# The first batch's front regrouped by heads and half tiles in an eight-batch linear-attention and mixer kernel

## The chip, the cores and the metric

The kernel runs on one core of a Trainium2 chip. The metric is the device time of one execution in microseconds; runs of one kernel agree within about 0.1%. In a profile PE is the matrix engine, PEld its weight loads, DVE, ACT and POOL are the vector, scalar and general-purpose engines, SP only issues DMAs. Engines run their own instruction lists in order and meet through semaphores.

## What is computed

Eight batches, eight heads, 576 rows, head dimension 64: linear attention with a cosine/sine weight, then a token mixer and a channel mixer. All inputs and the output are float32; the kernel multiplies in bf16.

```python
r = relu(q); q_p = concat([r*cos_w, r*sin_w], -1)   # the same for k: k_p
kv  = einsum('bhsf,bhsd->bhfd', k_p, v)
z   = sum(k_p, axis=2)
x   = einsum('bhsf,bhfd->bhsd', q_p, kv) / (einsum('bhsf,bhf->bhs', q_p, z) + 1e-6)
x   -> (B, 576, 512)                                  # heads side by side
u   = x + (relu(x^T @ w_tok1) @ w_tok2)^T             # 576 -> 256 -> 576
out = u + relu(u @ w_ch1) @ w_ch2                     # 512 -> 1536 -> 512
```

## The kernel before

The 576 rows of a batch are four chunks of 128 (`ci` 0 to 3, R = 4) and a tail of 64 rows; the tails of two batches share one tile of 128. For each batch there is a *front* (attention and token mixer) and a *channel* stage (`c_main` L540, matmuls with w_ch1, L546; `o_step` L572, matmuls with w_ch2, L579). The order of every engine is written out by hand. From batch 1 on, the pieces of a front are set between the steps of the channel stage of the batch before, by a list of (step, piece) that `pieces` (L461) makes: KS and QS make the features of k and q (L261 on ACT, L263 on DVE), V casts values to bf16 (L274 to L276), KV the product k_p^T v (L320), N the numerator (L359) and its division (L367 to L369), `u` the second token matmul (L406). In batch 2 and later the transposes of q run as DMA transposes on SP's queue (`q_trans_dma` L348, issue L350).

The front of batch 0 (`first_front`, L636) has nothing to hide behind. It goes, in PE's order:

- 12 filler matmuls (`busy`, L204: zeros times the identity into a tile nobody reads), then the transposes of q (L340) for heads 0 to 3 and then 4 to 7, each copied to SBUF by ACT (L344), then the tail of q;
- for k: features, two fillers, `ksum` (L285: eight one-column matmuls a chunk), chunk by chunk; ACT makes half of the features of chunks 2 and 3; then `ksum_out` (L293, ACT);
- `dens` (L302), the denominators of three chunks; `kv` for heads 0 to 3; `dens` of the other two; `kv` for heads 4 to 7. `kv_out` (L331) copies the low half on ACT and the high half on DVE;
- `num` (L359) with the division on DVE (L369, one instruction a chunk) two chunks ahead of `tok1` (L382, two matmuls a chunk); ACT casts w_tok1 (L207) and reorders w_tok2 (L210, L212) meanwhile;
- relu into B (L387, L389), the transposed u (L425, L433), its copies (L707), and the first channel matmuls (L556).

PSUM pools: `ps_mm` with four tiles of one bank, `ps_at` with two tiles of two banks. `kv` of each half takes a `ps_at` tile.

Loads. SP issues q heads 0-3 (L105), then the tail of q, k in two halves, the tail of k, v heads 0-3, the tail of v, v heads 4-7, w_tok1, w_tok2; ACT issues q heads 4-7 at the same time as SP's first. SP's and ACT's loads share eight semaphores in turn, so each load from the ninth on also waits until the load eight before it has landed. POOL issues the casting loads: the tail rows of w_tok1, then w_ch1 in four pieces (L188), the first of which waits for k's second half (L192). Batch 1's k, v and q (L736) wait for the second piece of w_ch1. w_ch2 comes in three pieces of four chunks (L196), which stand in POOL's list behind and between two casts of batch 1's values. Batch 2's loads of v and of all tails (L762, L763) are issued late in batch 0's channel stage and stand on SP ahead of two output stores and of batch 2's DMA transposes.

Of the kernel before, what the change touches and what calls it, by code (L numbers as in the profile page):

```python
# [16 lines left out]
def kernel(  # L17
# [87 lines left out]
    load_main(qt0, q, 0, HH, H, nc.scalar)  # L105
    load_tail(qtt0, q, 0)
    load_main(kt0, k, 0, 0, HH)
    k_done = load_main(kt0, k, 0, HH, H)
# [3 lines left out]
    load_main(vt0, v, 0, HH, H)  # L112
# [3 lines left out]
    w_tok1n = stage1[:, 0:R * D_tok].rearrange("p (r t) -> p r t", r=R)  # L116
    w_tok2n = stage2[:, 0:NT * S].rearrange("p (n s) -> p n s", n=NT)
    nc.sync.dma_start(out=w_tok1n, in_=moe_w_tok1[0:SM, :].rearrange("(p r) t -> p r t", r=R))
    nc.sync.dma_start(out=w_tok2n, in_=moe_w_tok2.rearrange("(n t) s -> t n s", t=P))
# [35 lines left out]
    v_augs, x_tails = [], []  # L155
    for i in range(2):
        va = const.tile([P, NSC, H, DP], BF16, name=f"v_aug{i}")
        nc.vector.memset(va[:, 0:R, :, D:D1], 1.0)
        nc.vector.memset(va[half(1 - i), R, :, :], 0.0)
        nc.vector.memset(va[half(i), R, :, D:D1], 1.0)  # L160
        v_augs.append(va)
        xt = const.tile([P, Dm], BF16, name=f"x_tail{i}")
        nc.vector.memset(xt[half(1 - i), :], 0.0)
        x_tails.append(xt)
# [15 lines left out]
    for t in (tail0.kp, tail0.qp):  # L180
        nc.gpsimd.memset(t[half(1)], 0.0)
    for g in range(2):
        nc.gpsimd.dma_start(out=w_tail1[half(g), :], in_=moe_w_tok1[SM:S, :])
# [8 lines left out]
    after(w_ch1_done[0], k_done)  # L192
    w_ch2_done = []
    def load_w_ch2(third):
        ki = third * NCH // 3
        w_ch2_done.append(nc.gpsimd.dma_start(  # L196
            out=w_ch2[:, ki:ki + 4, :],
            in_=moe_w_ch2[ki * P:(ki + 4) * P, :].rearrange("(n t) d -> t n d", t=P)))
# [10 lines left out]
    def permute_tok2(ki):  # L209
        nc.scalar.copy(w_tok2[:, ki, 0:SM].rearrange("t (r p) -> t r p", r=R),  # L210
                       w_tok2n[:, ki, 0:SM].rearrange("t (p r) -> t r p", r=R))
        nc.scalar.copy(w_tok2[:, ki, SM:].rearrange("t (g s) -> t g s", g=2),  # L212
                       w_tok2n[:, ki, None, SM:S].to_broadcast([P, 2, ST]))


    class Front:
        def __init__(self, b, res, tail):
            self.qt, self.vt, self.kt = io_tiles[b]
            self.va, self.xt = v_augs[b % 2], x_tails[b % 2]
            self.res, self.tail = res, tail  # L220
            self.rows = half(b % 2)


            self.alone = b < 2
            self.kp, self.qp = {}, {}

            self.qpT = once.tile([P, R * H, P], BF16, name="qpT")
            self.kv_sb = [twos.tile([P, HH, DP], BF16, name=f"kv_sb{g}") for g in range(2)]
            self.x = once.tile([P, R, Dm], BF16, name="x_sb")
# [65 lines left out]
        def dens(self, ci):  # L295

            if ci == 0:
                self.d_ps = ps_mm.tile([P, NSC * H], F32, name="d_ps", tag="mm")
                self.d_sb = small.tile([P, NSC * H, 1], F32, name="d_sb")
            for h in range(H):  # L300
                i = ci * H + h
                nc.tensor.matmul(self.d_ps[:, i:i + 1], self.qT_of(ci, h),  # L302
                                 self.ks_sb[:, h:h + 1], start=True, stop=True)

        def dens_out(self, lo, hi):
            nc.vector.tensor_scalar_add(self.d_sb[:, lo:hi, 0], self.d_ps[:, lo:hi], 1e-6)
            nc.vector.reciprocal(self.d_sb[:, lo:hi, 0], self.d_sb[:, lo:hi, 0])

        def kv(self, ci, halves=(0, 1)):
            if ci == 0 and not hasattr(self, "kv_ps"):  # L310
                self.kv_ps = {}
                if halves == (0, 1):
                    both = ps_at.tile([P, 2, 512], F32, name="kv_ps", tag="at")
                    self.kv_ps = {g: both[:, g, :] for g in range(2)}
            if ci == 0 and halves != (0, 1):
                for g in halves:
                    self.kv_ps[g] = ps_at.tile([P, 2, 512], F32, name="kv_ps", tag="at")[:, 0, :]
            for g in halves:
                for j in range(HH):
                    nc.tensor.matmul(self.kv_ps[g][:, j * DP:j * DP + D1],  # L320
                                     self.k_of(ci)[:, g * HH + j, :, :]
                                     .rearrange("p a b -> p (a b)"),
                                     self.va[:, ci, g * HH + j, 0:D1],
                                     start=(ci == 0 and j == 0),
                                     stop=(ci == NSC - 1 and j == HH - 1),
                                     skip_group_check=True)

        def kv_out(self, halves=(0, 1)):
            for g in halves:
                copy = nc.vector.tensor_copy if g else nc.scalar.copy  # L330
                copy(self.kv_sb[g][:, :, 0:D1],  # L331
                     self.kv_ps[g][:, 0:HH * DP]
                     .rearrange("p (j d) -> p j d", d=DP)[:, :, 0:D1])
# [13 lines left out]

        def q_trans_dma(self, ci):  # L348
            dst = self.qpT[:, ci * H:(ci + 1) * H, :] if ci < R else self.tail.qpT
            nc.sync.dma_start_transpose(out=dst,  # L350
                                        in_=self.q_of(ci).rearrange("p h a b -> p (h a b)"))

        def num(self, ci, fill=0, dens=False):
            num_ps = ps_at.tile([P, 2, 512], F32, name="num_ps", tag="at")
            if fill:
                busy(num_ps[:, 0, HH * DP:512], 1)
            for h in range(H):
                g, j = divmod(h, HH)
                nc.tensor.matmul(num_ps[:, g, j * DP:j * DP + D1], self.qT_of(ci, h),  # L359
                                 self.kv_sb[g][:, j, 0:D1], start=True, stop=True)  # L360
            rows = self.rows_of(ci)
            nv = num_ps[rows, :, 0:HH * DP].rearrange("p g (j d) -> p g j d", d=DP)
            if dens:
                den = self.d_sb[rows, ci * H:(ci + 1) * H, :].rearrange("p (g j) o -> p g j o", g=2)
            else:
# [3 lines left out]
            nc.vector.tensor_mul(  # L369
                self.x_of(ci)[rows].rearrange("p (g j d) -> p g j d", g=2, j=HH),  # L370
                nv[:, :, :, 0:D], den.to_broadcast([rows.stop - rows.start, 2, HH, D]))
# [89 lines left out]
        def pieces(self, b, before):  # L461
# [7 lines left out]
            if first:  # L469

                u, act, pool = before.tok2, nc.scalar, nc.gpsimd
                plan = [(4, KS, 0), (4, KS, 1), (5, u, 0, ps_at, False), (5, KS, 2, True),
                        (6, KS, 3, True), (6, u, 1, ps_at, False), (7, KS, R), (7, V, R, nc.vector), (8, V, 0, act),
                        (8, V, 2, pool), (8, load_w_ch2, 0), (8, V, 3, pool),
                        (8, load_w_ch2, 1), (8, load_w_ch2, 2),
                        (8, u, 2, None, False), (9, V, 1, act), (9, u, 3, None, False),
                        (9, QS, 0), (10, u, R, None, False)]
# [6 lines left out]
            else:  # L484
                plan = [(C + at, V, ci, nc.scalar)
                        for ci, at in enumerate((6, 6, 7, 7, 7) if late else (-1, -1, 0, 1, 2))]
# [10 lines left out]
                for at, side, ci in sides:  # L497
                    plan.append((C + at, side, ci))
                    if side == QS:
# [3 lines left out]
                         enumerate((7, 7, 8, 8, 8) if late else  # L503
# [28 lines left out]
    class Channel:  # L532
# [59 lines left out]
        def steps(self, done):  # L592
# [24 lines left out]
            if self.b == 0:  # L617

                for lo in range(0, NCH, 4):
                    for ci in (0, 1):  # L620
                        o_range(ci, lo, lo + 4)
# [14 lines left out]
    def first_front(f):  # L636
# [4 lines left out]
        busy(idle_ps, 12)  # L641
# [10 lines left out]
        f.q_side(R)  # L652
        f.q_trans(R, pool=ps_at)
        busy(idle_ps, 2)
        for ci in range(R):
            f.feature("k", ci, 0)
            f.feature("k", ci, 1, on_act=(ci > 1))
            busy(idle_ps, 2)
# [4 lines left out]
        busy(idle_ps, 1)  # L663
        for ci in range(R):
            if ci == 2:
                f.ksum_out()
            f.values(ci, nc.scalar, lo_heads)
        cast_tok1(0)
        f.values(R, nc.vector)
        for ci in range(R):  # L670
            f.values(ci, nc.vector, hi_heads)
        for ci in (0, 1, 2):
            f.dens(ci)
# [3 lines left out]
        for ci in (R, 3):  # L677
            f.dens(ci)
        f.dens_out(0, NSC * H)
        for ci in range(NSC):  # L680
            f.kv(ci, (1,))
        f.kv_out((1,))
        cast_tok1(1)
        for ki in range(NT):
            permute_tok2(ki)
# [3 lines left out]
        f.num(ORDER[0], fill=1, dens=True)  # L689
        f.num(ORDER[1], dens=True)  # L690
        for i, ci in enumerate(ORDER):
            if i + 2 < NSC:
# [55 lines left out]
    for b in range(B):  # L748
# [4 lines left out]
        for i, step in enumerate(steps):  # L753
# [5 lines left out]
            if b == 0 and i == NCH:  # L759
                load_batch(2, "kq", behind=w_ch2_done[1], tails=False)  # L760
            if b == 0 and i == NCH + 13:
                load_batch(2, "v", tails=False)  # L762
                load_batch(2, "kqv", main=False)  # L763
# [44 lines left out]
```

## Time and profile before

| what | us |
|---|---|
| median of 3 runs (range) | 269.88 (269.80 to 269.96) |
| the profiled execution, its time | 270.61 |
| its span, first to last instruction | 268.8 |
| PE busy in the span | 260.0 (97%), 2029 matmuls |
| DVE, ACT, POOL busy | 164.9, 129.9, 10.9 |
| first channel matmul (L556) starts | 24.45 |
| DMA: moved, mean rate | 53.68 MB, 200 GB/s |

The profiled execution takes 1.8 us outside its span, and is 0.7 us longer than the median. The page names the share of the span each engine was busy; a busy PE may be doing filler. The chain of waits says what released what, back from the last instruction; the timeline lists instructions with start, duration, engine, line and what the engine idled for; the windows give busy time by stretch. Starts are in us from the span's start. The durations of matmuls overlap their successors: spacing, not duration, is the cost of one.

### The profile page before, as it was taken

To read this page: it belongs to the slowest core of one execution; us is meant where nothing else is said; L and a number is where in the kernel's file an instruction comes from. 1 tells how busy PE (TensorE), PEld (TensorE's weight loads), DVE (VectorE), ACT (ScalarE), POOL (GpSimd) and SP (SyncE) were. 2 spreads that over 40 slices of the span, in tenths; PEclk is the share of its full clock that TensorE was granted. 3 is DMA by queue.
4 is the path that set the end of the run, shared out by engine and by line. 5 is a ranking of instruction groups with operands and counts; after the bars stand their busy time and mean duration, and the time that the engine had idled before them with its cause. 6 is when DMAs were issued, how large, how long until landed. Compare 5 with 4: busy or idle time off the path is not lost.

```text
span 268.8 us, 5101 instructions
## 1 busy us (share of the span) xinstructions
PE 260.0 (97%) x2029; PEld 139.2 (52%) x2050; DVE 164.9 (61%) x376; ACT 129.9 (48%) x228; POOL 10.9 (4%) x24
## 2 busy tenths in 40 slices
PE   7989999999999999999999999999999999999994
PEld 2565465455544455446644455446644455445543
DVE  6874798794366747777466747776565846720022
ACT  4954975528606272446606372546606362526400
POOL 6300220000000000000000000000000000000000
PEclk9999999999999999999999999999999999999999
DMA  6999999589999999469984989189974580180032
GB/s 217 342 277 275 333 162 285 211 210 253 179 316 289 251 208 319 146 166 266 182 307 117 287 207 355 54 179 254 229 261 117 156 120 0 53 202 3 2 107 88
DMA packets 91815, 53.68 MB, mean 200 GB/s; under 512 B 59408, under 2 KB 86928, under 8 KB 91792
## 3 DMA queue, kind: packets, MB, share of 16 engines
q1 hardware_dynamic: 88432, 49.62, 69.5%
q0 software_dynamic: 2832, 3.21, 7.2%
q10 hardware_dynamic: 528, 0.52, 0.6%
q8 instruction: 16, 0.26, 0.4%
q14 instruction: 7, 0.06, 0.1%
HBM read 35.85 MB, written 9.44 MB: 168 GB/s over the span
## 4 chain that ended last, share of the span: by engine, by line
PE 86%; DVE 6%; DMA 3%; ACT 3%; issue 1%; DVEq 0%; ACTq 0%
PE o_ps L579 33%; PE c_ps L546 25%; PE u_ps L406 7%; PE b_ps L382 6%; PE ct_ps L566 3%; PE kv_ps L320 3%; PE num_ps L359 3%; DVE x_sb L369 3%; DMA qt<-in_q_dram 2%; DVE qp L263 1%; ACT h1T L550 1%; PE qT_ps L340 1%; DMA qpT_tail<-qp_tail 1%; PE idle_ps L204 1%; ACT v_aug L274 1%; PE c_ps L556 1%
## 5 line engine op out<-in xcount | busy, mean ns | idle before, releaser
L579 PE MATMUL o_ps<-w_ch,h1T 128*128 128x512 bf16 (+1 forms) x380 | 92.6, 372 | 0.6
L546 PE MATMUL c_ps<-uT,w_ch 128*128 128x512 bf16 (+2 forms) x384 | 92.2, 372 | 0.1
L550 ACT ACTIVATE h1T<-c_ps 128x512 bf16<-128x512 f32 x93 | 55.5, 599 | 60.5 <-PE c_ps L546 60.1
L579 PEld LDWEIGHTS <-h1T 128*128 128x128 bf16 x396 | 37.3, 98 | 39.5 <-issue 0.2
L546 PEld LDWEIGHTS <-w_ch 128*128 128x128 bf16 x384 | 33.5, 97 | 29.5 <-issue 0.2
L584 DVE TENSOR_TENSOR o_sb<-o_ps,u_sb 128x512 f32<-128x512 f32 (+1 forms) x33 | 22.3, 674 | 29.5 <-PE o_ps L579 29.4
L409 DVE TENSOR_TENSOR u_sb<-u_ps,x_sb 128x512 f32<-128x512 f32 x32 | 21.7, 689 | 6.0 <-PE u_ps L406 5.6
L413 ACT CAST u_bf<-u_sb 128x512 bf16<-128x512 f32 x28 | 17.3, 620 | 16.7 <-DVE u_sb L409 16.7
L406 PE MATMUL u_ps<-B,w_tok 128*128 128x512 bf16 x79 | 22.4, 379 | 0.2
L387 ACT ACTIVATE B<-b_ps 128x512 bf16<-128x512 f32 x8 | 4.8, 598 | 33.7 <-PE b_ps L382 33.5
L369 DVE TENSOR_TENSOR x_sb<-num_ps,den 128x512 bf16<-128x512 f32 x28 | 19.4, 691 | 1.0
L566 PEld LDWEIGHTS <-w_ch 128*128 128x128 bf16 x192 | 14.0, 98 | 9.2
L382 PE MATMUL b_ps<-x_sb,w_tok 128*128 128x512 bf16 x63 | 17.7, 379 | 0.1
L263 DVE TENSOR_SCALAR kp<-kt,cos_t 128x512 bf16<-128x512 f32 x32 | 15.2, 481 | 3.8 <-DMA kt<-in_k_dram 3.8
L566 PE MATMUL ct_ps<-uT_tail,w_ch 128*128 128x128 bf16 x192 | 17.2, 219 | 0.0
L274 ACT CAST v_aug<-vt 128x512 bf16<-128x512 f32 (+1 forms) x30 | 16.8, 587 | 0.1
L263 DVE TENSOR_SCALAR qp<-qt,cos_t 128x512 bf16<-128x512 f32 (+1 forms) x35 | 15.9, 455 | 0.5 <-DMA qt<-in_q_dram 0.5
L263 DVE TENSOR_SCALAR qp<-qt,sin_t 128x512 bf16<-128x512 f32 (+1 forms) x35 | 15.9, 455 | 0.0
L359 PEld LDWEIGHTS <-qpT 128*128 128x128 bf16 x256 | 11.5, 98 | 6.1 <-issue 1.1
L584 DVE TENSOR_TENSOR o_sb<-o_ps,u_tail 128x512 f32<-128x512 f32 x4 | 2.8, 692 | 19.0 <-PE o_ps L579 19.0
L359 PE MATMUL num_ps<-kv_sb,qpT 128*128 128x65 bf16 x256 | 13.0, 193 | 1.3 <-DVE x_sb L369 0.5
L331 DVE CAST kv_sb<-kv_ps 128x260 bf16<-128x260 f32 x8 | 3.5, 433 | 16.6 <-ACT kv_sb L331 16.5
(93 smaller groups left out, 228.6 us busy)
## 6 DMA issues: line engine op xcount, KB each, us to landing
out_dram<-o_sb SPq DMA_DIRECT2D x31, 256.0 KB, 2.9
kt<-in_k_dram SPq DMA_DIRECT2D x7, 1024.0 KB, 6.6
vt<-in_v_dram SPq DMA_DIRECT2D x7, 1024.0 KB, 6.6
qt<-in_q_dram SPq DMA_DIRECT2D x7, 1024.0 KB, 8.4
w_ch<-in_moe_w_ch_dram POOLq DMA_DIRECT2D x4, 384.0 KB, 10.2
w_ch<-in_moe_w_ch_dram POOLq DMA_DIRECT2D x3, 512.0 KB, 7.5
out_dram<-o_sb SPq DMA_DIRECT2D x10, 128.0 KB, 2.3
qtt<-in_q_dram SPq DMA_DIRECT2D x8, 128.0 KB, 5.3
```

The source lines that it names most:

```text
L263: nc.vector.tensor_scalar(o_ap, i_ap, scalar1=w, scalar2=0.0, op0=ALU.mult, op1=ALU.max)
L274: nc.scalar.copy(dst, src)
L359: nc.tensor.matmul(num_ps[:, g, j * DP:j * DP + D1], self.qT_of(ci, h), self.kv_sb[g][:, j, 0:D1], start=True, stop=True)
L369: nc.vector.tensor_mul(self.x_of(ci)[rows].rearrange("p (g j d) -> p g j d", g=2, j=HH), nv[:, :, :, 0:D], den.to_broadcast([rows.stop - r ...
L382: nc.tensor.matmul(self.b1_ps[mi], w, self.x_of(ci), start=(ci == ORDER[0]), stop=(ci == ORDER[-1]))
L406: nc.tensor.matmul(u_ps, w_tok2[:, ki, ci * P:(ci + 1) * P], self.B1[:, ki, :], start=(ki == 0), stop=(ki == NT - 1))
L409: nc.vector.tensor_add(u, u_ps[rows], self.x_of(ci)[rows])
L546: nc.tensor.matmul(c_ps[:, lo:hi], w_ch1[:, ki, mi * P:(mi + 1) * P], uT[:, lo // P:hi // P, ki, :], start=(ki == 0), stop=(ki == NCC - 1))
L550: nc.scalar.activation(self.h1T[:, mi, :], c_ps, AF.Relu)
L566: nc.tensor.matmul(self.ct_ps[:, mi % R, :], w_ch1[:, ki, mi * P:(mi + 1) * P], self.tail.uT[:, ki, :], start=(mi % R == 0 and ki == 0), s ...
L579: nc.tensor.matmul(o_ps, h, w_ch2[:, ki, cols], start=ki == 0, stop=ki == NCH - 1)
L584: nc.vector.tensor_add(o_sb, o_ps, u)
```

## The change

The front of batch 0, the loads around it, and the slots of some pieces of batches 1 and 2 are changed; all arithmetic stays. Cut to its core, by parts:

```diff
@@ loads of batch 0
     load_main(qt0, q, 0, 0, HH)
-    load_main(qt0, q, 0, HH, H, nc.scalar)
-    load_tail(qtt0, q, 0)
+    load_main(qt0, q, 0, HH, H)
     load_main(kt0, k, 0, 0, HH)
-    k_done = load_main(kt0, k, 0, HH, H)
+    load_main(kt0, k, 0, HH, H)
     load_tail(ktt0, k, 0)
     load_main(vt0, v, 0, 0, HH)
     load_tail(vtt0, v, 0)
-    load_main(vt0, v, 0, HH, H)
+    load_main(vt0, v, 0, HH, HH + HH // 2)
+    load_main(vt0, v, 0, HH + HH // 2, H)
+    qkv_done = load_tail(qtt0, q, 0)
...
+    for g in range(2):
+        nc.sync.dma_start(out=w_tail1n[half(g), :], in_=moe_w_tok1[SM:S, :])
...
-    for g in range(2):
-        nc.gpsimd.dma_start(out=w_tail1[half(g), :], in_=moe_w_tok1[SM:S, :])
...
-    after(w_ch1_done[0], k_done)
+    after(w_ch1_done[0], qkv_done)
@@ pieces of batch 1 (first), slots
-                plan = [(4, KS, 0), (4, KS, 1), (5, u, 0, ps_at, False), (5, KS, 2, True),
-                        (6, KS, 3, True), (6, u, 1, ps_at, False), (7, KS, R), (7, V, R, nc.vector), (8, V, 0, act),
-                        (8, V, 2, pool), (8, load_w_ch2, 0), (8, V, 3, pool),
-                        (8, load_w_ch2, 1), (8, load_w_ch2, 2),
-                        (8, u, 2, None, False), (9, V, 1, act), (9, u, 3, None, False),
-                        (9, QS, 0), (10, u, R, None, False)]
+                plan = [(4, u, 0, ps_at, False), (5, u, 1, ps_at, False), (6, u, 2, None, False),
+                        (6, KS, 0), (6, KS, 1), (7, u, 3, None, False), (7, KS, 2, True),
+                        (8, u, R, None, False), (8, KS, 3, True), (9, KS, R),
+                        (9, V, R, nc.vector), (9, V, 0, act),
+                        (10, V, 2, pool), (10, load_w_ch2, 0, 2), (10, V, 3, pool),
+                        (10, load_w_ch2, 2, 4), (10, load_w_ch2, 4, 8),
+                        (10, load_w_ch2, 8, NCH), (10, V, 1, act), (11, QS, 0, True)]
@@ pieces of batch 2 (late): V at steps 6,6,7,7,7 -> 4,5,6,6,7; KV at 7,7,8,8,8 -> 6,7,7,8,8
@@ o_step order of batch 0: chunks 0 and 1 in turn, by 4 -> by 2 of the 12 k-blocks
@@ first_front
-        busy(idle_ps, 12)
+        busy(idle_ps, 10)
...
-        f.q_side(R)
-        f.q_trans(R, pool=ps_at)
-        busy(idle_ps, 2)
-        for ci in range(R):
+        for heads in (lo_heads, hi_heads):
+            f.feature("k", 0, 0, heads)
+            f.feature("k", 0, 1, heads)
+        busy(idle_ps, 4)
+        f.ksum(0)
+        for ci in range(1, R):
             f.feature("k", ci, 0)
-            f.feature("k", ci, 1, on_act=(ci > 1))
-            busy(idle_ps, 2)
+            f.feature("k", ci, 1, on_act=True)
+            busy(idle_ps, 1 + min(ci, 2))
             f.ksum(ci)
         f.k_side(R)
         busy(idle_ps, 2)
         f.ksum(R)
...
+        f.ksum_out()
+        busy(idle_ps, 2)
         for ci in range(R):
-            f.values(ci, nc.scalar, lo_heads)
-        cast_tok1(0)
+            f.values(ci, nc.vector if ci < 2 else nc.scalar, lo_heads)
         f.values(R, nc.vector)
         for ci in range(R):
-            f.values(ci, nc.vector, hi_heads)
-        for ci in (0, 1, 2):
-            f.dens(ci)
+            f.values(ci, nc.vector if ci < 2 else nc.scalar, mid_heads)
+        main = f.dens(range(R))
+        f.dens_out(*main)
+        busy(idle_ps, 1)
         for ci in range(NSC):
             f.kv(ci, (0,))
         f.kv_out((0,))
-        for ci in (R, 3):
-            f.dens(ci)
-        f.dens_out(0, NSC * H)
+        for ci in range(R):
+            f.values(ci, nc.vector, top_heads)
+        busy(f.kv_ps[1], 2)
+        for ci in ORDER[:2]:
+            f.num(ci, dens=True, halves=(0,), pool=ps_mm)
         for ci in range(NSC):
             f.kv(ci, (1,))
-        f.kv_out((1,))
-        cast_tok1(1)
-        for ki in range(NT):
-            permute_tok2(ki)
+        f.feature("q", R, 1, on_act=True)
+        f.kv_out((1,), on_act=(1,))
+        f.feature("q", R, 0)
+        for ci in ORDER[:2]:
+            f.num(ci, dens=True, halves=(1,), fill=2)
+        f.q_trans_tail_first()
+        for mi in range(NT):
+            cast_tok1(mi)
+        permute_tok2(0, nc.scalar.copy)
+        nc.gpsimd.tensor_copy(w_tail1, w_tail1n)
+        permute_tok2(1, nc.gpsimd.tensor_copy)
+        fill_fixed(1, nc.gpsimd)
...
-        f.num(ORDER[0], fill=1, dens=True)
-        f.num(ORDER[1], dens=True)
         for i, ci in enumerate(ORDER):
-            if i + 2 < NSC:
+            if i == 0:
+                f.num(ORDER[2], dens=True, fill=2)
+                tail = f.dens([R])
+                f.dens_out(*tail)
+            elif i + 2 < NSC:
                 f.num(ORDER[i + 2], dens=True)
@@ loads of batch 2
             if b == 0 and i == NCH + 13:
                 load_batch(2, "v", tails=False)
-                load_batch(2, "kqv", main=False)
+                load_batch(2, "k", main=False)
+            if b == 1 and i in (2, 3):
+                load_batch(2, "vq"[i - 2], main=False)
```

`mid_heads` are heads 4 and 5, `top_heads` 6 and 7. `q_trans_tail_first` is new: eight transposes of the 64 tail rows of q into a `ps_mm` tile, then one copy on ACT. `fill_fixed(1, ...)` holds the fixed values of the second value tile, which DVE set before. The second `kv` half is accumulated in the second bank of the other `ps_at` tile, and its copy goes to ACT. On SP, batch 2's order becomes: v, tails of k, two output stores, two DMA transposes of q, tails of v, a transpose, tails of q, a transpose, the transpose of q's tail.

## The prediction

> **What bounds the kernel now.** I read the page's chain first, then the windows, then the timeline of PE, and last what feeds PE where it idles. The chain of what ended last is PE's:
>
> ```profile
> PE 86%; DVE 6%; DMA 3%; ACT 3%; issue 1%; DVEq 0%; ACTq 0%
> ```
>
> The windows (length, busy PE, PEld, DVE, ACT, POOL, clock, DMA share, GB/s) tell where PE is not full:
>
> ```profile
> 18.00:22.00 4.00, 3.41 (x48) 2.10 (x46) 3.23 (x5) 2.72 (x5) 0.00 (x0) 1.00 1.17 209
> 27.00:37.00 10.00, 9.95 (x48) 4.54 (x48) 8.31 (x16) 8.47 (x15) 3.55 (x5) 1.00 1.08 282
> 70.00:86.00 16.00, 15.24 (x115) 7.80 (x115) 10.25 (x23) 5.95 (x11) 0.00 (x0) 1.00 0.98 295
> ```
>
> From 22 to 65 and after 76 PE has no holes, so a microsecond by which the front ends later stays to the end. Two places count: the front up to the first c_ps matmul (24.45), and batch 2's front near 65 to 75. The front is a chain through all engines (the timeline; start, duration):
>
> ```profile
> 11.61 0.35 PE L285 MATMUL ks_ps<-ones,kp 128*128 128x1 bf16 x8
> ...
> 14.68 0.17 ACT L293 CAST ks_sb<-ks_ps 128x8 bf16<-128x8 f32 x1 [0.89 <-PE ks_ps L285]
> ...
> 15.46 0.62 ACT L207 CAST w_tok<-u_sb 128x512 bf16<-128x512 f32 x1
> ...
> 16.51 0.65 PE L320 MATMUL kv_ps<-v_aug,kp 128*128 128x65 bf16 x16
> ...
> 17.32 0.43 DVE L331 CAST kv_sb<-kv_ps 128x260 bf16<-128x260 f32 x1
> ...
> 18.12 1.89 DVE L369 TENSOR_TENSOR x_sb<-num_ps,d_sb 128x512 bf16<-128x512 f32 x3 [0.37 <-PE num_ps L359]
> ...
> 19.32 0.38 PE L382 MATMUL b_ps<-x_sb,w_tok 128*128 128x512 bf16 x1
> ...
> 21.40 0.59 PE L382 MATMUL b_ps<-x_sb,w_tok 128*128 128x512 bf16 x2
> ```
>
> w_tok1 is cast by 17.2, long before the first b_ps at 19.32, which follows the first x. The last b_ps pair ends near 22.0.
>
> In batch 2's front SP is late (timeline of SP, ACT, DVE, PE):
>
> ```profile
> 63.81 7.74 SPq L350 DMA_TRANSPOSE qpT<-qp  x4
> 66.93 0.62 ACT L274 CAST v_aug<-vtt 64x512 bf16<-64x512 f32 x1
> 68.46 0.43 DVE L331 CAST kv_sb<-kv_ps 128x260 bf16<-128x260 f32 x1 [3.34 <-ACT kv_sb L331]
> 70.62 0.42 PE L359 MATMUL num_ps<-kv_sb,qpT 128*128 128x65 bf16 x8 [0.44 <-ACT h1T L550]
> 74.57 0.42 PE L359 MATMUL num_ps<-kv_sb,qpT_tail 128*128 128x65 bf16 x8 [0.22 <-DMA qpT_tail<-qp_tail]
> ```
>
> The 0.44 ends when the first transpose lands (70.57), so ACT is named wrongly; the 0.22 is the tail's. With 0.12 and 0.07 at kv (65.5, 67.5) and 0.08 at 59.4, 0.9 us of holes lie here, and no more can be won.
>
> **The front, step by step.** Start: k's second half lands at 10.57 and DVE resumes at 10.66. Ahead of it the queue loses q's tail, which took 0.50 (5.94 to 6.44), and the two casting loads of w_tok1's tail. I take 0.7 earlier, 9.95; bounds 10.66 (the transfers shared the engines anyway) and 9.3 (both and the tail's 0.4 on DVE). q's first half, now alone in the queue, lands earlier than 5.31, but nothing is gained by that: DVE is through q before k's second half either way. DVE makes k's chunk 0 in four pieces; the last two, 0.26 apart as for q, end at 10.5. Then PE: five ksum groups at 0.20 and ten fillers at 0.215 (spacing in the rows 13.04 to 13.67) are 3.15; ACT's three sines at 0.76 end at 12.3, so the fillers set the pace, and the last ksum completes at about 13.85 against 14.65. That is 0.8 gained; ks_sb is there at 14.07.
>
> Then it is given back. dens now has 32 columns ahead of kv, at 0.025 each 0.8, and a filler 0.2: kv low runs 15.1 to 15.75 (before 15.50). Its copy on ACT takes 0.39, to 16.3 (two fillers lie under it); eight low num matmuls at 0.0325, 0.26; kv high starts at 16.65 against 16.51, and kv_sb high is there at 17.8 against 17.75. The values lie beside this: ACT's four end near 15.3, DVE's last top heads at 16.2.
>
> Next the list of ACT decides. Behind kv_sb high it has the copy of the tail's transposes, and only behind that both w_tok1 casts. PE does num high twice (0.26), fillers of 192 columns (0.2) and eight transposes at 0.055 (0.44) first, with latencies to 18.8. The copy takes 0.51 (the row of L344: 8 in 4.08), to 19.35; the first cast 0.62, to 20.0; the second 0.5, to 20.5. So the first b_ps starts at 20.0, not 19.32. Behind the second b_ps PE has the tail's num (0.26, to 21.05), two b_ps (0.43), the last num (0.26, to 21.75), x of chunk 3 on DVE 0.69, and the last pair ends at 22.9 to 23.1. DVE's halved x (4 at about 0.35 instead of 2 at 0.63) puts x of chunks 0 and 1 at 18.8, 0.6 before it was, and wins nothing because w_tok1 is late. The b_ps chain ends **1.05 later**. Bounds: +0.2 (k at 9.3, waits shorter) and +1.8 (k at 10.66). POOL's casts and memsets (w_tail1, half of w_tok2, second v_aug) cost nothing: needed at 22 and 37, POOL is idle after 17.4; cover gone, a cast of 512 columns costs 0.6 to 0.8 (its v_aug rows), and the strided one on ACT 1.11.
>
> **DMAs behind it.** w_ch1 now waits for the last of q, k, v, about 13.9, so POOL issues at 14.2 instead of 10.85. Its packets began 4.3 after the issue (15.1); with that, 18.4, behind the end of w_tok2, and alone at 0.207 MB/us (19 to 22 in the trace) the second piece lands at 23.0 instead of 21.37: 1.6 later. Its use by c_ps (kb 2, 25.7) is covered. Batch 1's loads, the casts and w_ch2 hang on it: w_ch2's last third landed at 44.90 and its step ran at 45.95, slack 1.05. So PE would be held to at least +0.55 there, hidden behind a front that is 1.05 late. The other end is 0 (w_ch1 at once beside w_tok). [...] Batch 1's u before its k features moves the same work on DVE, PE and ACT; qp's sine of chunk 0 goes to ACT behind h1T (37.8), and its transposes wait up to 0.3 (they ran at 38.19). I take 0.1.
>
> **Batch 2.** Seen from SP at 58.5: v, k tails, two stores, two transposes now go out at 59.7 instead of 63.8, which takes away the 0.44. But v's tail loads stand behind two transposes and q's tail behind three. By the old spacing (tails 0.45 each, stores 0.8 each, transposes 0.9 each, v done at 61.2) v's tails move at about 66 and land at 67.3, q's at 69.2. ACT's cast of v's tail ran at 66.93 and the tail's kv on PE at 67.60: 0.3 late. q's tail features stand ahead of kv_sb on DVE, so kv_sb comes at 70.4 instead of 68.9, and num at about 70.5 where PE is at 70.18. That end of the range is -0.9 plus 0.7, about -0.2. The transposes of before did not run at 0.9, though: the first, behind stores, took until 70.57, with packets standing still from 66.1 to 68.0 and again from 68.9 to 70.4. One such stop of 1.5 to 1.9 ahead of v's tails puts kv's tail 1.5 to 2 late; a second ahead of q's tails adds 1 to 2 at num. That end is +3.5. Two more changes between copies and transposes are made than before, so I take one stop partly hidden: **+1.0**.
>
> **Sum.** 1.05 + 0.1 + 1.0 = 2.1. On the profiled execution's 270.61 this is 272.7; that lies 0.73 above the median of 269.88, so 272.0 for the median.
>
> **Rivals.** *Transposes stand still* (both stops, +3.5): 269.88 + 1.15 + 3.5 = 274.5. For it: two stops in one such sequence. Against: they may stand elsewhere. *Batch 2 clean*: +1.15 - 0.2 to -0.8, 270.2 to 270.8; for it, the late transposes are the named wait. *Faster*: the earlier transposes of batch 2 give back 0.8, and decide where the front loses less than 0.25, that is with the first b_ps before 19.5: k at 9.3 and waits of ACT's list 0.3 shorter; +0.2 + 0.1 - 0.8 = -0.5 to -1.0, 269.1. Against it: w_tok1's casts behind the tail's copy, and the 0.55 from w_ch2. *The fillers do not do what they are for*: PE's spacing stayed 0.215 after holes of 0.55 and 0.54 before, so no clock is won; this is in the forecast.
>
> **How the numbers follow.** Forecast (271.1 to 273.2) 0.45; stops 0.23 (273.2 to 276); clean 0.19, of which half within 0.2%; faster 0.13. The range leaves out the ends: 269.3 to 275.0. Within 0.2% (0.54 us) is about what a measurement of this kernel can tell from no change. Faster 0.13, same 0.12, slower 0.75.
>
> **What shows it.** ks_sb near 14.1, kv_sb high near 17.8, first b_ps near 20.0 behind w_tok1's cast, first c_ps near 25.5; w_ch1's second landing 21 to 23; in batch 2 the first num without a transpose's wait but v's tail cast after 67.2 from its landing. Wrong if b_ps starts before 19.5, or if batch 2's tails land by 66.5.

## The result, and the profile after

The changed kernel takes 277.89 us (median of 4 runs, 277.03 to 278.20) against 269.84 beside it: a ratio of 1.030 (95% interval 1.027 to 1.032), slower by 8.0 us where 2.1 were forecast. The profiled execution took 278.20, its span 276.1. The kernel before, run again beside the experiments, spread from 269.28 to 270.95 (one run 271.92), more than the 0.1% said above; so small differences below are read by their intervals.

The chain of what ended last no longer belongs to PE alone:

```profile
PE 68%; DMA 15%; SPq 7%; DVE 6%; issue 1%; POOL 1%; POOLq 0%; ACT 0%; DVEq 0%
```

PE had 86% of it; DMA and SP's queue now hold 22%. The longest pieces of that chain up to batch 1 (start, duration, what):

```profile
10.33 5.86 DMA qtt<-in_q_dram
17.32 6.26 DMA w_ch<-in_moe_w_ch_dram
24.68 10.27 DMA vt<-in_v_dram
37.84 9.62 DMA w_ch<-in_moe_w_ch_dram
```

q's tail releases w_ch1, this releases batch 1's loads, and these w_ch2: loads in a row. The windows (columns as in the prediction's):

```profile
18.00:22.00 4.00, 2.84 (x66) 2.49 (x63) 2.86 (x8) 2.61 (x6) 3.94 (x9) 1.00 1.07 157
27.00:37.00 10.00, 9.95 (x47) 4.53 (x47) 4.57 (x8) 5.81 (x11) 1.93 (x3) 1.00 1.06 345
37.00:46.00 9.00, 8.16 (x107) 5.47 (x107) 8.81 (x21) 8.07 (x13) 2.36 (x4) 1.00 0.98 149
70.00:86.00 16.00, 12.40 (x139) 7.66 (x139) 6.89 (x19) 6.44 (x13) 0.00 (x0) 1.00 0.80 205
```

The kernel before, from 37 to 46:

```profile
37.00:46.00 9.00, 8.89 (x140) 6.64 (x141) 8.27 (x24) 6.27 (x8) 0.00 (x0) 1.00 1.09 224
```

PE loses in three places: from 18 to 22 it is busy for 2.84 instead of 3.41, from 37 to 46 it is busy for 8.16 instead of 8.89, and from 70 to 86 it is busy for 12.40 instead of 15.24. Setting each instruction of ACT against the same one of the kernel before gives where the time was lost: 2.57 up to the first c_ps, the first channel matmul (24.45 to 27.02), another 2.0 in batch 1 (4.6 late at 58), another 2.8 in batch 2 (7.4 late from 86 on), and nothing after that. The two profiled executions differ by 7.6, the medians by 8.0. The prediction had 1.05, 0.1 and 1.0.

**Front.** Timeline of DVE and PE:

```profile
9.69 0.35 DVE L265 TENSOR_SCALAR kp<-kt,cos_t 128x256 bf16<-128x256 f32 x1 [1.34 <-DMA kt<-in_k_dram]
...
11.34 0.35 DVE L265 TENSOR_SCALAR kp<-kt,cos_t 128x256 bf16<-128x256 f32 x1 [1.04 <-DMA kt<-in_k_dram]
...
12.02 0.25 PE L287 MATMUL ks_ps<-ones,kp 128*128 128x1 bf16 x4 [1.41 <-DVE kp L265]
...
21.88 0.39 PE L394 MATMUL b_ps<-x_sb,w_tok 128*128 128x512 bf16 x1 [0.61 <-ACT w_tok L209]
```

k's second half lands at 11.32, not 9.95, so DVE and then PE stand still; b_ps waits for the casts of w_tok1, as forecast. (The b_ps shown is the second; the first has a weight load at 21.36 and no matmul record. In the kernel before, 19.32 is likewise the second: the weight loads begin at 19.08.)

**Batch 1.** Timeline of DVE, POOL and PE:

```profile
35.16 0.80 DVE L265 TENSOR_SCALAR kp<-kt,cos_t 128x512 bf16<-128x512 f32 x1
...
35.07 0.61 POOL L278 CAST v_aug<-vt 128x512 bf16<-128x512 f32 x1 [12.45 <-DMA vt<-in_v_dram]
...
41.37 0.40 PE L321 MATMUL kv_ps<-v_aug,kp_tail 128*128 128x65 bf16 x8 [0.30 <-DVE v_aug L278]
41.98 1.21 PE L341 MATMUL qT_ps<-ident,qp 128*128 128x128 bf16 x14 [0.21 <-DVE qp L265]
```

k landed at 31.51, but its first DVE feature runs at 35.16, behind three pieces of u, and takes 0.80 instead of 0.48 while POOL casts v and issues w_ch2. Everything behind it on DVE is late, kv and qT wait.

**Batch 2.** Timeline of SP, ACT, DVE and PE:

```profile
64.62 5.27 SPq L360 DMA_TRANSPOSE qpT<-qp  x2
69.94 1.29 SPq L92 DMA_DIRECT2D vtt<-in_v_dram  x2
71.33 2.10 SPq L360 DMA_TRANSPOSE qpT<-qp  x1
73.48 1.28 SPq L92 DMA_DIRECT2D qtt<-in_q_dram  x2
...
73.72 0.62 ACT L276 CAST v_aug<-vtt 64x512 bf16<-64x512 f32 x1 [1.65 <-DMA vtt<-in_v_dram]
...
74.39 0.40 PE L321 MATMUL kv_ps<-v_aug,kp_tail 128*128 128x65 bf16 x8 [1.55 <-ACT v_aug L276]
...
77.30 0.49 DVE L265 TENSOR_SCALAR qp_tail<-qtt,cos_t 128x512 bf16<-128x512 f32 x1 [7.67 <-DMA qtt<-in_q_dram]
...
78.58 0.28 PE L369 MATMUL num_ps<-kv_sb,qpT 128*128 128x65 bf16 x4 [1.50 <-DVE kv_sb L332]
```

Two transposes hold SP for 5.27 (what holds it so long is open), so v's tail is only asked for at 69.94; one more holds it for 2.10 ahead of q's tail. v's tail keeps kv waiting, and q's tail keeps DVE, behind which stands the copy of kv for which num waits.

### The profile page after: what moved, and what is told of

The parts are those of the page before. It is cut to its first block, busy times and chain, and to the rows that moved or that the text cites. A ratio compares the mean times of both kernels' runs of the same rounds, so it can differ in the third digit from the quotient of the medians.

```text
span 276.1 us, 5134 instructions
## 1 busy us (share of the span) xinstructions
PE 262.2 (95%) x2037; PEld 140.5 (51%) x2059; DVE 163.9 (59%) x378; ACT 130.1 (47%) x230; POOL 12.9 (5%) x30
## 4 chain that ended last, share of the span: by engine, by line
PE 68%; DMA 15%; SPq 7%; DVE 6%; issue 1%; POOL 1%; POOLq 0%; ACT 0%; DVEq 0%
PE o_ps L592 30%; PE c_ps L559 20%; DMA w_ch<-in_moe_w_ch_dram 6%; PE b_ps L394 5%; PE u_ps L418 5%; DMA vt<-in_v_dram 4%; DMA qtt<-in_q_dram 3%; PE ct_ps L579 3%; SPq L92 2%; SPq L86 2%; DVE x_sb L382 2%; PE kv_ps L321 2%; DMA ktt<-in_k_dram 2%; PE num_ps L369 2%; SPq L360 1%
## 5 line engine op out<-in xcount | busy, mean ns | idle before, releaser
L265 DVE TENSOR_SCALAR kp<-kt,cos_t 128x512 bf16<-128x512 f32 (+1 forms) x33 | 16.0, 490 | 2.4 <-DMA kt<-in_k_dram 2.4
L276 ACT CAST v_aug<-vt 128x512 bf16<-128x512 f32 (+2 forms) x30 | 16.5, 581 | 1.2 <-DMA vt<-in_v_dram 1.2
L265 DVE TENSOR_SCALAR kp<-kt,sin_t 128x512 bf16<-128x512 f32 (+1 forms) x28 | 13.7, 490 | 0.0
```

Source lines behind the costliest of these rows:

```text
L265: nc.vector.tensor_scalar(o_ap, i_ap, scalar1=w, scalar2=0.0, op0=ALU.mult, op1=ALU.max)
```

## Experiments

### The stages apart

*front_only*: batch 1's plan, w_ch2's pieces and all of batch 2 as before. *batch2_back*: only batch 2 as before. *batch2_only* and *batch1_only*: the kernel before with that part alone.

```diff
 front_only, against the changed kernel; batch2_back has the last two pairs alone
-plan = [(4, u, 0, ps_at, False), (5, u, 1, ps_at, False), ...
+plan = [(4, KS, 0), (4, KS, 1), (5, u, 0, ps_at, False), ...
-enumerate((4, 5, 6, 6, 7) if late ...   # V; KV likewise
+enumerate((6, 6, 7, 7, 7) if late ...
-load_batch(2, "k", main=False) ... load_batch(2, "vq"[i - 2], main=False)
+load_batch(2, "kqv", main=False)
```

> The changed kernel with batch 1's plan, w_ch2 in thirds and batch 2's slots and tail loads as they were before: only the front and its loads are changed. Theory A (the three shares that the two traces show are caused each in its own stage: front 2.6, batch 1 2.0, batch 2 2.8): 269.8 + 2.6 = 272.4, and the first c_ps near 27.0. Theory B (the front's later loads push w_ch1, w_ch2 and batch 1's pieces behind, so that a part of the 2.0 and the 2.8 comes with the front): 273.5 to 275, with PE's holes in batch 1 behind w_ch2 or v's landing.

> The changed kernel with batch 2's slots (V, KV) and its tail loads as they were before; front and batch 1 stay changed. Theory A: 277.9 - 2.8 = 275.1, with batch 2's holes back at about 0.9 us. Theory B (batch 2's holes come from arriving late, whatever the order there): 276.5 to 278.

> The kernel before with batch 2's slots and tail loads changed alone. Theory A: 269.8 + 2.8 = 272.6. Theory B: 270.0 to 271.0, since v and the tails come on time behind an early front.

> The kernel before with batch 1's plan changed alone (u of batch 0 ahead of the k features, w_ch2 in four pieces, the output matmuls of batch 0 in steps of two). Theory A: 269.8 + 2.0 = 271.8. Theory B: 269.8 to 270.5, as loads are on time here.

> The changed kernel once more. In its first profile k's second half landed at 11.32 and the first c_ps ran 2.57 later than before; with the same front in front_only and batch2_back it landed at 9.78 and 9.76, and the first c_ps was 1.0 to 1.3 later. Theory A (the late landing belongs to that one execution): k's second half near 9.8, first c_ps near 25.5, time 276.5. Rival (it belongs to this program): near 11.3 again, first c_ps near 27.0, time 277 to 278.

| kernel | median us | before beside it | difference |
|---|---|---|---|
| front_only | 272.45 | 269.82 | +2.63 |
| batch2_back | 273.38 | 269.82 | +3.56 |
| batch2_only | 273.37 | 269.82 | +3.55 |
| batch1_only | 272.06 | 269.82 | +2.24 |
| changed kernel again | 276.79 | 269.71 | +7.08 |

Each part costs time by itself. Batch 2's part costs 3.55 on the kernel before and 276.79 - 273.38 = 3.4 on top of the rest: it does not come from arriving late, and Theory B falls there; it is more than the 2.8 that the two traces showed. Front and batch 1 do not add: 2.63 and 2.24 alone, 3.56 together, so that both theories missed batch2_back's time. That front_only met Theory A's 272.4 is luck: its first c_ps ran at 25.48, 1.03 late, not near 27.0, and the rest was lost in batch 1. There batch 1's old plan meets later loads (k at 31.71 instead of 28.41), and u waits on DVE behind k's features and v's cast, as PE shows:

```profile
38.18 0.59 PE L419 MATMUL u_ps<-B,w_tok 128*128 128x512 bf16 x2 [1.31 <-DVE u_sb L422]
```

batch2_back has no such hole, because u stands first there; it has smaller ones at kv and qT instead. So the new plan costs 0.9 on top of the late front, but 2.24 alone. In front_only's profile k landed at 9.78 and the first c_ps ran at 25.48: the forecast's 9.95 and 25.5. The changed kernel run again had k at 10.51 and the first c_ps some 1.8 late instead of 2.57, and took 1.1 less. That lies between the theory and its rival: k's landing is no fixed part of the change but varies, and the first profile showed a late one.

### Batch 2

```diff
 slots_only: the kernel before with V at (4, 5, 6, 6, 7) and KV at (6, 7, 7, 8, 8)
 vtail_early, against batch2_only
-load_batch(2, "k", main=False)
+load_batch(2, "kv", main=False)          # only q's tail between the transposes
 tails_together, against batch2_only
-if b == 1 and i in (2, 3): load_batch(2, "vq"[i - 2], main=False)
+if b == 1 and i == 2: load_batch(2, "vq", main=False)
 qtail_behind_kv, against batch2_only
-(5, KS, R), (6, QS, R)
+(5, KS, R), (9, QS, R)
```

> The kernel before with only batch 2's V and KV slots moved ahead by one step or two (V to 4, 5, 6, 6, 7 and KV to 6, 7, 7, 8, 8); the tails' loads stay as they were. Theory A (the 3.5 of batch2_only come from the tails that wait behind transposes): 269.8 to 270.3, no hole over 0.6 at kv. Rival (the slots ask for v before it has landed at 62): 271 to 273 with kv's holes as in batch2_only.

270.12 against 269.71, ratio 1.002 (1.000 to 1.004), no hole at kv: the slots cost nothing that can be told.

> Batch 2's change alone as in batch2_only, but v's tail loads are put in front of the transposes again, with k's; only q's tail loads stay between the transposes. Theory A (each pair of tail loads is late by what the two transposes ahead of it take, and each costs its own hole): kv's holes of 2.2 go, num's hole of 1.9 stays; 271.5. Rival (the tails are late however they stand, since the queue is full): within 0.5 of batch2_only, 273 to 273.5.

273.74 (272.02 to 274.00), where 271.5 was expected. kv's holes go, but num's grows. DVE and PE of vtail_early, in the execution of 272.02:

```profile
71.21 0.49 DVE L263 TENSOR_SCALAR qp_tail<-qtt,cos_t 128x512 bf16<-128x512 f32 x1 [7.05 <-DMA qtt<-in_q_dram]
...
72.49 0.28 PE L359 MATMUL num_ps<-kv_sb,qpT 128*128 128x65 bf16 x4 [2.75 <-DVE kv_sb L331]
```

PE, no longer held at kv, comes to num earlier and waits there for the same tail. The other three runs, 1.6 to 2 longer, have no profile, but their mean granted clock is 0.991 to 0.994. A stretch of 3.4 us at half clock would give 0.994 and add 1.7 (an estimate from the 3.41 us of gate_back below), so the lower clock can account for most of the difference. What lowered it is not shown: the profiled execution kept 1.00 over its hole of 2.75.

> batch2_only with v's and q's tail loads together behind the first two transposes instead of one pair behind two and one behind three. Theory A (what a tail waits for is the issue of each transpose ahead of it on SP's queue, 2 to 3 us apiece): kv's holes stay near 2.2, q's tail lands some 2 earlier (70.5 instead of 72.5), num's hole of 1.9 shrinks to 0.3 or less; 271.5 to 272. Rival (each change between loads and transposes costs a stop, wherever it stands): one change less, but the same order of landing; 272.5 to 273.4.

272.15 (271.53 to 273.24). num's hole is 0.29, kv's stay (0.51 and 1.55). q's tail landed at 72.14, not 70.5, but this execution, the longest of the ten, came to batch 2 some 1.2 later than batch2_only's. By the hole and the median the rival falls.

> batch2_only with the q tail's features of batch 2 put behind the copy of kv on DVE (slot 9 instead of 6); the loads stay late. Theory A (num's hole of 1.9 is DVE's copy of kv, queued behind features that wait for q's tail): that hole goes, kv's holes of 2.2 stay, and the tail's transpose is late next by at most 0.9; 271.8 to 272.5. Rival (num waits for its transposes anyway): the hole stays, named after qpT; 273.2 to 273.5.

272.55. PE's largest holes (kv has one of 0.51 ahead of them):

```profile
69.99 0.40 PE L320 MATMUL kv_ps<-v_aug,kp_tail 128*128 128x65 bf16 x8 [1.73 <-ACT v_aug L274]
76.75 0.42 PE L359 MATMUL num_ps<-kv_sb,qpT_tail 128*128 128x65 bf16 x8 [0.62 <-DMA qpT_tail<-qp_tail]
```

num's hole of 1.90 is gone though q's tail is as late as before: DVE's order made it. The tail's transpose is late next, by 0.62. The causes of the two large holes are shown: v's tail late behind two transposes (1.65 of the 2.2 at kv in batch2_only), and kv's copy queued on DVE behind q's tail (1.9 at num). The other 0.51 at kv is not the tail's: v's main load landed 6.4 after its issue instead of 5.5 (slots_only), so ACT's casts began late. Taking away one hole gave back only 0.8 to 1.4 of the 3.55 (in vtail_early only the run at full clock), since the next wait took its place; slots_only, with the loads as before, has neither.

### Batch 1

```diff
 wch2_only: the kernel before, k's features still ahead of u
-load_w_ch2, 0 ... 1 ... 2                # thirds
+load_w_ch2, 0, 2 ... 2, 4 ... 4, 8 ... 8, NCH
-for lo in range(0, NCH, 4): ... o_range(ci, lo, lo + 4)
+for lo in range(0, NCH, 2): ... o_range(ci, lo, lo + 2)
```

> The kernel before with only w_ch2's loads in four pieces (2, 2, 4, 4 of twelve) instead of three, and batch 0's output matmuls in steps of two; batch 1's plan keeps its k features ahead of u. Theory A (the 2.25 of batch1_only come from k's features, which stand behind u on DVE and ACT): 269.5 to 270.3, no holes at batch 1's kv and qT. Rival (w_ch2's fourth piece and steps of two cost it): 271 to 272.

270.69 against 269.71 (ratio 1.004, 1.002 to 1.006), and no hole at batch 1's kv and qT. batch1_only differs from it by the order of u and k's features and by later slots of the casts of v and of w_ch2's loads, and takes 1.3 more (2.24 - 0.98). Its profile has holes of 0.23 and 0.21 at kv and qT and several under 0.15; over kv, qT and num PE's spacing is 1.4 longer than in the kernel before. DVE of batch1_only, where k landed at 28.42:

```profile
30.53 0.69 DVE L408 TENSOR_TENSOR u_sb<-u_ps,x_sb 128x512 f32<-128x512 f32 x1 [0.55 <-PE u_ps L405]
31.82 0.69 DVE L408 TENSOR_TENSOR u_sb<-u_ps,x_sb 128x512 f32<-128x512 f32 x1 [0.60 <-PE u_ps L405]
32.43 0.52 DVE L262 TENSOR_SCALAR kp<-kt,cos_t 128x512 bf16<-128x512 f32 x1
```

In the kernel before, the first of k's features ran at 28.43. The other 1.0 is measured with the pieces of w_ch2 alone (0.6 to 1.6 by the interval); the profiled execution, the shortest of eight, doesn't show it, so where it is lost is open.

### The front

```diff
 gate_back, against front_only
-after(w_ch1_done[0], qkv_done)
+after(w_ch1_done[0], k_done)
 fill_less, against batch2_back
-busy(idle_ps, 1 + min(ci, 2)) ... busy(idle_ps, 2) ... busy(idle_ps, 2)
+busy(idle_ps, 1) ... busy(idle_ps, 1) ... busy(idle_ps, 1)
 after_qact, against the changed kernel; front_qact, against gate_back
-load_main(qt0, q, 0, HH, H)
+load_main(qt0, q, 0, HH, H, nc.scalar)
```

> front_only with w_ch1's loads held back behind k's second half, as they were before, instead of behind the last of q, k and v. Theory A (the hole of 1.3 at batch 1's u_ps in front_only comes from w_ch1, which moves 0.21 MB per us whatever is beside it and now begins 3 us later): w_ch1 ends near 25 to 25.5, v of batch 1 lands near 32 to 33, the hole goes; 271.0 to 271.6. Rival (w_ch1 beside v takes from v what it gains): first c_ps 0.5 to 1 later than in front_only; 272 to 273.

272.08, but from 270.62 to 274.65. In the profiled execution (274.65) k landed at 11.97, PE stood still for 1.5 at ksum, and its granted clock, the third column from the end, fell:

```profile
10.00:13.00 3.00, 1.14 (x12) 0.45 (x11) 1.62 (x6) 1.35 (x3) 0.73 (x1) 1.00 1.13 263
13.00:16.00 3.00, 3.00 (x24) 1.38 (x23) 2.71 (x10) 1.28 (x2) 2.86 (x4) 0.54 1.09 291
```

It was 0.50 for 3.41 us, from 13.27 on. Batch 1's hole is gone, but this execution doesn't show Theory A's reason: PE came 3.6 later than in front_only, w_ch1 ended at 28.62 and v landed at 35.64, no earlier than front_only's 35.54. front_qact below, with k on time, shows it: w_ch1 ends at 25.34, v lands at 31.93, and there is no hole. The shortest runs here, near 271, are what Theory A expected. The theory's 0.21 MB per us is the rate of w_ch1 alone (kernel before, 19 to 20); beside w_tok2, from 16 to 17, w_ch1's queue moved 0.16 MB.

> batch2_back (changed front and batch 1, batch 2 as before) with seven of the fillers in k's part left away: one instead of two or three ahead of each ksum, one instead of two around ksum's copy. Theory A (the fillers set the pace there, at 0.215 apiece): ks_sb at 13.0 instead of 14.0, first c_ps 0.6 to 0.9 earlier, 272.5 to 272.8 against 273.4. Rival (they keep the clock or hide another wait): granted clock under 1.00 or longer spacing of matmuls, or a hole where the fillers were, and 273.2 to 273.6.

The four runs lie between 272.95 and 277.08, too far apart to compare. Theory A was not put to the test: k landed at 11.71 in the profiled execution, PE stood still for 1.4, and the clock was 0.50 from 13.0 to 19.8. Two of the four runs have a mean clock of 0.981 and 0.988; batch2_back's have 0.999 and more.

> The changed kernel with one line undone: q's high heads are loaded from ACT's queue again, beside those on SP's. Theory A (with q's halves in one queue, k's second half lands anywhere from 9.8 to 12.0; in the seven profiles with two queues it landed from 9.8 to 10.6): k by 10.6, no hole over 0.6 ahead of ksum, first c_ps 1.0 to 1.8 later than before's 24.45, 276.0 to 276.9. Rival (the late landing comes from the rest of the order, with q's tail behind v): k between 10.5 and 11.5 again, 277 to 278.

277.92 (275.96 to 278.17), the changed kernel's own time, though k landed at 9.13. Two things took the gain. q's first half, no longer alone, lands at 5.52 instead of 4.47, and DVE's features start that much later, so that ks_sb comes 0.98 earlier (14.29) where k came 2.19 earlier. Then PE has holes of 0.35 and less around x and w_tok1, and the clock falls (the one run that kept it at 1.00 is the 275.96, Theory A's time):

```profile
18.00:21.00 3.00, 2.03 (x37) 1.56 (x36) 2.61 (x6) 1.59 (x4) 2.64 (x6) 1.00 1.15 207
21.00:24.00 3.00, 2.87 (x22) 1.58 (x22) 1.15 (x3) 1.47 (x3) 0.00 (x0) 0.52 1.16 213
```

It was 0.50 for 3.41 us, from 21.15 to 24.56; PE was busy for 2.4 of the 3.41 us before the drop. What lowered it is not shown.

> gate_back with q's high heads on ACT's queue. gate_back's ten runs spread from 270.6 to 274.7, and in the profiled one k landed at 11.97, PE stood still for 1.5 and its granted clock was 0.50 from 13.5 to 16.5. Theory A: k by 10.6, clock 1.00 throughout, all runs within 1.0 of each other, median 270.8 to 271.4. Rival (k's landing has another cause): a spread of 3 us or more again, clock under 1.00 in some runs.

272.00 (271.20 to 274.60): k at 9.01 in the profiled execution, with clock 1.00, but two of six runs have a mean clock of 0.992 to 0.994. So k is early with q's high heads on ACT's queue, but the spread stays.

```diff
 front_cast, against front_qact; in first_front
+for mi in range(NT): cast_tok1(mi)
 f.q_trans_tail_first()
-for mi in range(NT): cast_tok1(mi)
 ...                                      # dens([R]) moves from i == 0 to i == 1
 front_cast_fill: front_cast with fill_less's edit
 kact_cast_fill and kact_cast: these two fronts, q's halves on SP again, and
+k_done = load_main(kt0, k, 0, HH, H, nc.scalar)   # behind theta's sines
```

> front_qact with w_tok1's two casts ahead of the copy of the tail's transposes on ACT, and the tail's dens one step later on PE. Theory A (the first b_ps waits for these casts behind that copy): first b_ps near 19.3 instead of 19.8, its holes of 0.47 gone, first c_ps 0.3 to 0.5 earlier, 270.4 to 271.0. Rival (x of chunk 0 or the landing of w_tok1 holds b_ps as well): no difference to front_qact beyond 0.2.

270.75 (270.25 to 271.61): 1.2 less than front_qact. The holes at b_ps are gone, the first c_ps is 0.64 earlier in the profiles, and all ten runs have clock 1.00. That copy ahead of the casts was a cost of time (the tail's dens moved with it). Whether it also cost the clock, in front_qact's two runs of six, is not shown.

> front_qact_cast with seven fillers of k's part left away, as in fill_less. Theory A (with k on time the fillers set the pace there, and no hole is long enough to lower the clock): ks_sb at 13.0, first c_ps another 0.5 to 0.8 earlier, clock 1.00, 269.8 to 270.4, about what the kernel before takes. Rival (without them the clock falls, or v's landing and its casts hold kv): clock under 1.00 or 270.4 to 271.2.

270.12 (269.52 to 272.17) against 269.67, ratio 1.002 (1.000 to 1.005): the first c_ps another 0.55 earlier. From k's landing to ks_sb it is 4.70 instead of front_cast's 5.39, so the fillers did set the pace, for 0.7 of the 1.5 that seven of them take. The two runs above 272 have a clock of 0.994. (The expectation's front_qact_cast is front_cast.) This is the best front that was tried, and it is not below the kernel before.

> front_cast_fill with q's two halves in SP's queue again and k's high heads loaded from ACT's queue, behind the two sines of theta (issued near 3.4). Theory A (two streams, one after the other for q, then side by side for k, keep the transfers at full rate, and q's first half is not shared): q's first half near 4.5 instead of 5.5, k's second by 9.2, first c_ps 0.5 to 0.9 earlier than in front_cast_fill, so 269.2 to 269.7, the first below the kernel before. Rival (whatever slowed the single queue from 5 to 8 slows this too): k's second half past 9.8, first c_ps no earlier, 270 or more, in some runs with the clock under 1.00.

> The same with the seven fillers of k's part kept. Theory A (the fillers set the pace when k is on time): 0.4 to 0.8 slower than e17, 269.8 to 270.4, with no run under clock 1.00. Rival (they keep the clock, which e17 loses): e17's runs spread by 2 us or more and its median lies above this one's.

kact_cast_fill (e17) takes 272.67 (270.98 to 274.53), kact_cast (e18) 272.36 (271.35 to 273.91). k's second half lands at 10.55 and 11.21, not by 9.2: Theory A falls. Between the two medians nothing can be told, but the clock differs: four of e17's six runs have a mean of 0.979 to 0.987, one of e18's six 0.991. Taken together, 8 of 20 runs without the seven fillers (fill_less, front_cast_fill, e17) have a mean clock under 0.995, and 1 of 20 with them (batch2_back, front_cast, e18). So the rival, that the fillers keep the clock, is likely; it is not shown, since k's landing differed too and fill_less and batch2_back ran on two chips.

The transfers' rate from 5 to 8 us tells the fronts apart, for the kernel before, the changed one and after_qact:

```profile
5.00:8.00 3.00, 2.44 (x23) 1.26 (x22) 2.58 (x10) 2.57 (x5) 0.00 (x0) 1.00 1.07 343
```

```profile
5.00:8.00 3.00, 2.97 (x32) 1.88 (x31) 3.00 (x13) 2.97 (x7) 0.00 (x0) 1.00 0.90 287
```

```profile
5.00:8.00 3.00, 1.73 (x20) 1.10 (x20) 2.38 (x10) 2.36 (x5) 0.00 (x0) 1.00 1.08 381
```

| q's high heads | profiles | GB/s, 5 to 8 us | k's second half lands |
|---|---|---|---|
| ACT's queue, q's tail ahead of k (before) | 8 | 343 to 357 | 9.83 to 10.60 |
| SP's queue behind the low heads (in two of them k's on ACT's) | 8 | 257 to 336 | 9.76 to 11.97 |
| ACT's queue, q's tail behind v | 4 | 379 to 383 | 8.82 to 9.15 |

The queue of q's high heads has an effect: on one chip, from which all four profiles of the last row come, k landed at 9.76 and 9.78 with one queue (front_only, batch2_back) and at 8.82 to 9.15 with two. SP also issues k's loads 0.5 earlier there, which may be part of it. Why the transfers slacken after q when both halves stand in one queue is open, and so are the landings after 10.5. But for the changed kernel's 11.32, whose chip is not known, they come from other chips (10.51 on one, 11.71 and 11.97 on the next, 10.55 and 11.21 on a third), where the last row's order was not run.

## Why the prediction was wrong

The sign was right, and two of the three places: batch 1 was not counted as one. All three terms were too small. Even their upper ends, 1.8 + 0.1 + 3.5 = 5.4, fall short of the 8.0.

1. **k's landing.** The step that failed is "I take 0.7 earlier, 9.95; bounds 10.66 and 9.3". It was taken from what leaves the queue; that q's high heads come into the queue was judged only by q itself. k landed at 9.76 to 11.97, at 11.32 in the profile, outside the bounds: 1.37 of the 1.5 by which the front's term was short. One queue instead of two accounts for 0.6 to 1.0 of such a delay; the rest of the 11.32 is open, and in the second profile it was 10.51. The rest of the front's sum held: from k's landing to the first c_ps it had 15.55 (9.95 to 25.5), and 15.7 were measured both in front_only (9.78 to 25.48) and in the changed kernel (11.32 to 27.02). So did its critical step, the first b_ps 10.05 after k: 10.04 in front_only. w_tok1's casts behind the tail's copy were a true cost, shown by front_cast.
2. **Batch 1.** "I take 0.1": the same work in another order was taken to cost nothing. Alone, the plan costs 2.24: 1.3 for the order and slots, as DVE runs in its order and stands idle between the pieces of u (0.55 and 0.60 in batch1_only) while k, landed, waits; 1.0 for the pieces of w_ch2, not found in a trace. On top of the changed front it costs 0.9.
3. **Batch 2.** "+1.0" came from "tails 0.45 each, stores 0.8 each, transposes 0.9 each", spacings of landings in a full queue. What a tail behind a transpose waits for is SP, which issues in order: two transposes held it for 5.27, one for 2.10. The prediction's own row of SP had four in 7.74, which is 1.9 apiece. In batch2_only v's tail landed at 68.9 and q's at 72.5, not 67.3 and 69.2; from issue to landing the tails took 2.7 to 3.8, no longer than v's before (3.0 to 4.0), so all of the delay lies ahead of the issue. The mechanism, kv's copy behind q's tail on DVE, was named and right; its size was not, and the part costs 3.4 to 3.55. The rival *Transposes stand still* had this size, +3.5, and both holes, but for another reason, so its number is in part luck: the DMA engines did not stand still over their packets, they ran dry because SP asked late (busy share 0.64 from 70 to 76 in batch2_only, 0.92 in the kernel before).

w_ch1's packets began 1.6 after its issue (16.49 to 18.05), not 4.3; what held them for 4.3 in the kernel before is not shown. The issue itself came at 16.49, not at 14.2, since the gate's loads were late (q's tail landed at 16.19), and w_ch1's second piece landed at 23.58 where 21 to 23 was forecast.

That the fillers win no clock was right for the changed kernel's profile (1.00 throughout) and said too broadly: in other fronts the clock was 0.50 after PE's holes (for 3.41 us in gate_back, 6.83 in fill_less), and it was below 0.995 more often without the seven fillers (8 runs of 20 against 1).

## What to carry to other kernels

On a queue that issues in order, price a moved load by how long the instructions ahead of it hold the issuer, not by the spacing at which they land: here two transposes held SP for 5.27, where 0.9 apiece was forecast. The same work in another order is not free by itself: look for an in-order engine that will wait on a late input while ready work stands behind it (1.3 for batch1_only's order and slots). Price a load that enters a queue as well as one that leaves it: k landed 0.6 to 1.0 later with q's high heads in its queue.

## What the runs showed of the hardware

- PE's granted clock fell to 0.50 after holes of 1.4 to 1.5 us, for 3.41 us in gate_back and 6.83 in fill_less, and for 3.41 us in after_qact, where PE was busy for 2.4 of the 3.41 us before the drop. Other holes left it at 1.00: 1.41 in the changed kernel, 1.65 and 1.90 in batch2_only, 2.75 in vtail_early. No run shows what decides it. The time of a front with holes varied: gate_back's ten runs lie from 270.62 to 274.65.
- The same order of loads gave k's landing anywhere from 9.76 to 11.97 when q's halves shared SP's queue: 9.76 and 9.78 on one chip, 11.71 and 11.97 on another.
- DVE's features of 512 columns took up to 0.83 instead of 0.48 at times when POOL cast v or issued w_ch2 (0.80 at 35.16 in the changed kernel, 0.83 at 32.87 in batch1_only). Whether POOL is the cause is not shown.
